# Whole-row gate and up weights in place of 512-column blocks, in the feed-forward tail of a decode kernel

## The chip, the cores and the metric

The kernel runs on one core of a Trainium2 chip. The metric is the time of one execution on the device in microseconds (us). Before the change the median of 4 runs is 473.97 us, with runs from 472.04 to 476.5. The profile is of one execution with a span of 470.3 us.

## The reference

The program is one decode step (one new token for each of 8 sequences) of a transformer block whose layer norms are modulated by a condition vector. It has two halves: attention over a cache of keys and values, and a gated feed-forward network (FFN). Cut to what matters:

```python
# B=8 tokens, D=1024, 32 query heads on 4 K/V heads, cache length 8192, head size 128, F=3584
mod = silu(c) @ w_mod                              # six vectors: sa, ca, ga, sb, cb, gb
h = layernorm(x) * (1 + ca) + sa
q = h @ wq
p = softmax(q @ k_cache^T * 128**-0.5)             # per batch and head
x = x + ga * ((p @ v_cache) @ wo)
h = layernorm(x) * (1 + cb) + sb
gate = h @ W_gate                                  # [8, 1024] @ [1024, 3584]
up = h @ W_up                                      # [8, 1024] @ [1024, 3584]
x = x + gb * ((relu(gate) * up) @ W_down)          # [8, 3584] @ [3584, 1024]
```

All large arrays are bf16. The caches are 32 pairs (8 sequences times 4 K/V heads) of a 2 MB K tile and a 2 MB V tile. W_gate, W_up and W_down have 7.34 MB each. Everything is read once: 185.6 MB.

## The kernel before

The engines run side by side and meet at semaphores. One queue, that of SyncE (SP), issues all loads in program order; a wait on it holds back every later load.

The attention loop goes over the 32 pairs. For each, PE transposes the K tile in 8 rounds (`T_round`, line 633), ACT and DVE copy the result out of PSUM, PE multiplies it with the query (`A_part`), DVE and ACT make the softmax, and PE multiplies with V (`D_step`, line 669). K and V have two slots each:

```python
def dma_v(i):
    b, g = pair_bg[i]
    s = i % NKV
    if i >= NKV:
        sp.wait_ge(ev_pv.sem, i - NKV + 1)            # D_step(i-2) done
    ...
    ev_dma_v[s].mark(sp.dma_start(V_sb[s], vsrc))

def dma_k(i):
    ...
    if i >= NKV:
        sp.wait_ge(ev_tround.sem, 8 * (i - NKV) + 8)  # transposes of i-2 done
    ev_dma_kt[s].mark(sp.dma_start(Kp_sb[s], ksrc))

for i in range(NPR):
    dma_k(i)
    if i >= 1:
        dma_v(i - 1)
    if i == NPR - 1:
        dma_v(i)
    if i == 1 and DO_MODB:
        dma_wmodB()
    if FULL and i % B == 3:
        dma_wo(g)
while ffn_issued[0] < len(ffn_blocks):                # after the last V
    dma_ffn(ffn_issued[0])
    ffn_issued[0] += 1
```

SBUF is laid out by hand in one arena of 192 KB per partition: RA (32 KB, output projection), RB (64 KB, first the query weights, then the second part of w_mod, which PE has used up early in the attention loop), RC (64 KB, the K and V slots), RKT (16 KB, the transposed K) and RD (16 KB, free).

The FFN weights are 21 blocks of 1 MB in the order gate, up, down for each of seven groups of 512 hidden columns. Each block has a slot of 8 KB per partition and a wait for whatever used the slot:

```python
if kind == "G":
    src = B_W_gate[:, fb * 512:(fb + 1) * 512].rearrange("(c p) f -> p c f", p=128)
elif kind == "U":
    src = B_W_up[:, fb * 512:(fb + 1) * 512].rearrange("(c p) f -> p c f", p=128)
else:
    src = B_W_down[fb * 512:(fb + 1) * 512, :].rearrange("(f p) d -> p f d", p=128)
ev_dma_ffn[blk].mark(sp.dma_start(ffn_view(blk), src))
```

PE works through the groups as they arrive, with gate and up of one group ahead of down of the group before. The weights are the stationary operand and the 8 tokens the moving one:

```python
def gate_up(fb):                                     # line 750
    for kind, coff in (("G", 0), ("U", 32)):
        pe.wait_ge(ev_dma_ffn[(kind, fb)].sem, 16)
        for f4 in range(4):
            for cc in range(NCH):                    # NCH = 8 chunks of the 1024 rows
                pe.matmul(PS[:, coff + f4 * B:...], wv[:, cc, f4 * 128:(f4 + 1) * 128],
                          h2T[:, cc, :], start=(cc == 0), stop=(cc == NCH - 1))
for fb in range(NFB + 1):                            # NFB = 7
    if fb < NFB:
        gate_up(fb)
    if fb >= 1:
        down(fb - 1)                                 # line 765, 32 matmuls
```

ACT applies the relu to each group's gate (line 419), DVE multiplies it with up (line 571) and adds up the results of `down` (line 565). At the end DVE makes the sum with the residual, PE transposes it, ACT copies it and SP stores it.

Of the kernel before, what the change touches and what calls it, by code (L numbers as in the profile page):

```python
# [4 lines left out]
F32 = mybir.dt.float32  # L5
ACTF = mybir.ActivationFunctionType
ALU = mybir.AluOpType
AX = mybir.AxisListType

B = 8  # L10
D = 1024
# [4 lines left out]
FF = 3584  # L16
REP = HQ // HKV
NCH = D // 128
NP = HKV * B
# [3 lines left out]
NFB = FF // 512  # L23
# [19 lines left out]
def bass_adaLN_cond__gqa_block_cached__glu_gated_reglu__decode_kernel(  # L43
# [15 lines left out]
    NPR = NP if FULL else DEBUG_NP  # L59
# [3 lines left out]
    KB = 1024  # L63
# [17 lines left out]
    RA = 0  # L81
    RB = 32 * KB
    RC = 96 * KB
    RKT = 160 * KB
    RD = 176 * KB
    NKV = 2
# [12 lines left out]

    ffn_blocks = []  # L100
    for fb in range(NFB):
        for kind in ("G", "U", "D"):
            ffn_blocks.append((kind, fb))
    last0 = max(i for i in range(NP) if i % NKV == 0)
    last1 = max(i for i in range(NP) if i % NKV == 1)
    ffn_slot_of = {}
    ffn_region_wait = {}
    tail_regions = [
        (KV_SLOT[0], ("T", last0)), (KV_SLOT[0] + 8 * KB, ("T", last0)),
        (KV_SLOT[1], ("T", last1)), (KV_SLOT[1] + 8 * KB, ("T", last1)),  # L110
        (RKT, ("A", NP - 1)), (RKT + 8 * KB, ("A", NP - 1)),
        (KV_SLOT[0] + 16 * KB, ("D", last0)), (KV_SLOT[0] + 24 * KB, ("D", last0)),
        (KV_SLOT[1] + 16 * KB, ("D", last1)), (KV_SLOT[1] + 24 * KB, ("D", last1)),
    ]
    for k, blk in enumerate(ffn_blocks):
        if k < 8:
            ffn_slot_of[blk] = RB + k * 8 * KB
            ffn_region_wait[blk] = ("modb", None)
        elif k < 10:
            ffn_slot_of[blk] = RD + (k - 8) * 8 * KB  # L120
            ffn_region_wait[blk] = ("free", None)
        elif k < 12:
            ffn_slot_of[blk] = RA + (k - 10) * 8 * KB
            ffn_region_wait[blk] = ("w", 3)
        else:
            off, wt = tail_regions[k - 12]
            ffn_slot_of[blk] = off
            ffn_region_wait[blk] = wt

    def ffn_view(blk):  # L130
        kind, fb = blk
        off = ffn_slot_of[blk]
        if kind == "D":
            return aview(off, [4, D])
        return aview(off, [NCH, 512])

    identb = nc.alloc_sbuf_tensor("identb", [128, 128], BF16)
# [29 lines left out]
    x1T = nc.alloc_sbuf_tensor("x1T", [128, NCH, B], F32)  # L167
    grelu = [nc.alloc_sbuf_tensor(f"grelu{k}", [128, 4, B], F32) for k in range(2)]
    hhT = nc.alloc_sbuf_tensor("hhT", [128, FF // 128, B], BF16)
# [10 lines left out]
    PS_W2 = nc.alloc_psum_tensor("psW2", [128, 512], F32)  # L180
    GU_BANK = [PS_W1, PS_W2]
    Y_OFF = 384
# [8 lines left out]
    ev_dma_wo = [Ev(nc, f"ev_dma_wo{h}", 16) for h in range(2)]  # L191
    ev_dma_ffn = {blk: Ev(nc, f"ev_dma_ffn_{blk[0]}{blk[1]}", 16) for blk in ffn_blocks}
    ev_out = Ev(nc, "ev_out", 16)
# [79 lines left out]
    with nc.Block() as block:  # L273
# [15 lines left out]
        def _(sp):  # L289
# [14 lines left out]

            ffn_issued = [0]

            def dma_ffn(k):
                blk = ffn_blocks[k]
                kind, fb = blk
                wk, wv = ffn_region_wait[blk]  # L310
                if wk == "modb":
                    sp.wait_ge(ev_pe_misc.sem, PE_MISC_MODB)
                elif wk == "free":
                    pass
                elif wk == "w":
                    sp.wait_ge(ev_w.sem, wv)
                elif wk == "T":
                    sp.wait_ge(ev_tround.sem, 8 * wv + 8)
                elif wk == "A":
                    sp.wait_ge(ev_qk.sem, wv + 1)  # L320
                else:
                    sp.wait_ge(ev_pv.sem, wv + 1)
                if kind == "G":
                    src = B_W_gate[:, fb * 512:(fb + 1) * 512].rearrange("(c p) f -> p c f", p=128)
                elif kind == "U":
                    src = B_W_up[:, fb * 512:(fb + 1) * 512].rearrange("(c p) f -> p c f", p=128)
                else:
                    src = B_W_down[fb * 512:(fb + 1) * 512, :].rearrange("(f p) d -> p f d", p=128)
                ev_dma_ffn[blk].mark(sp.dma_start(ffn_view(blk), src))  # L329

# [24 lines left out]
            for i in range(NPR):  # L355
                b, g = pair_bg[i]
                dma_k(i)
                if i >= 1:
                    dma_v(i - 1)
                if i == NPR - 1:  # L360
                    dma_v(i)
                if i == 1 and DO_MODB:
                    dma_wmodB()
                if FULL:
                    if i % B == 3:
                        dma_wo(g)
            if FULL:
                while ffn_issued[0] < len(ffn_blocks):
                    dma_ffn(ffn_issued[0])
                    ffn_issued[0] += 1  # L370
                sp.wait_ge(ev_act_misc.sem, ACT_MISC_OUT)
                ev_out.mark(sp.dma_start(out.rearrange("t o (c p) -> (t o c) p", p=128), out_sb[0:B * NCH, :]))
            else:
                if NPR > 0:
                    sp.wait_ge(ev_ao.sem, NPR)
                else:
                    sp.wait_ge(ev_dve_misc.sem, DVE_MISC_QT)
                if DO_MODB:
                    sp.wait_ge(ev_act_misc.sem, ACT_MISC_MODB)
                ev_out.mark(sp.dma_start(out.rearrange("b o d -> (b o) d"), xc_nl[0:B, :]))  # L380
# [3 lines left out]
        def _(act):  # L384
# [29 lines left out]
            ln_sqrt(2)  # L414
            for fb in range(NFB):
                act.wait_ge(ev_ffn1.sem, 2 * fb + 2)
                if fb >= 2:
                    act.wait_ge(ev_hh.sem, fb - 1)
                ins = act.activation(grelu[fb % 2][:, :, :], GU_BANK[fb % 2][:, 0:32].rearrange("p (f t) -> p f t", t=B),  # L419
                                     ACTF.Relu)  # L420
                assert ev_relu.mark(ins) == fb + 1
            act.wait_ge(ev_pe_misc.sem, PE_MISC_FIN)
# [3 lines left out]
        def _(dve):  # L426
# [131 lines left out]
            def o2_acc(fb):  # L558
# [7 lines left out]
                assert ev_o2.mark(ins_) == fb + 1  # L566

            for fb in range(NFB):
                dve.wait_ge(ev_ffn1.sem, 2 * fb + 2)
                dve.wait_ge(ev_relu.sem, fb + 1)  # L570
                ins = dve.tensor_tensor(hhT[:, fb * 4:(fb + 1) * 4, :], grelu[fb % 2][:, :, :],  # L571
                                        GU_BANK[fb % 2][:, 32:64].rearrange("p (f t) -> p f t", t=B), ALU.mult)
                assert ev_hh.mark(ins) == fb + 1
                if fb >= 1:
                    o2_acc(fb - 1)
            o2_acc(NFB - 1)

# [7 lines left out]
        def _(pe):  # L585
# [152 lines left out]

            def gate_up(fb):
                PS = GU_BANK[fb % 2]  # L740
                if fb >= 2:
                    pe.wait_ge(ev_hh.sem, fb - 1)
                for kind, coff in (("G", 0), ("U", 32)):
                    blk = (kind, fb)
                    pe.wait_ge(ev_dma_ffn[blk].sem, 16)
                    wv = ffn_view(blk)
                    ins_ = None
                    for f4 in range(4):
                        for cc in range(NCH):
                            ins_ = pe.matmul(PS[:, coff + f4 * B:coff + (f4 + 1) * B],  # L750
                                             wv[:, cc, f4 * 128:(f4 + 1) * 128],
                                             h2T[:, cc, :], start=(cc == 0), stop=(cc == NCH - 1))
                    assert ev_ffn1.mark(ins_) == 2 * fb + (1 if kind == "G" else 2)

            def down(fb):
                blk = ("D", fb)
                pe.wait_ge(ev_dma_ffn[blk].sem, 16)
                pe.wait_ge(ev_hh.sem, fb + 1)
                if fb >= 2:
                    pe.wait_ge(ev_o2.sem, fb - 1)  # L760
                wv = ffn_view(blk)
                ins_ = None
                for dc in range(NCH):
                    for f4 in range(4):
                        ins_ = pe.matmul(PS_S[fb % 2][:, dc * B:(dc + 1) * B], wv[:, f4, dc * 128:(dc + 1) * 128],
                                         hhT[:, fb * 4 + f4, :], start=(f4 == 0), stop=(f4 == 3))
                assert ev_ffn2.mark(ins_) == fb + 1

            for fb in range(NFB + 1):
                if fb < NFB:  # L770
                    gate_up(fb)
                if fb >= 1:
                    down(fb - 1)

# [33 lines left out]
```

## Time and profile before

| | |
|---|---|
| median of 4 runs | 473.97 us |
| span of the profiled execution | 470.3 us |
| PE busy | 357.2 us (76%) |
| DVE busy | 216.2 us (46%) |
| ACT busy | 122.9 us (26%) |
| bytes moved | 186.73 MB, mean 397 GB/s |
| transposes of K, line 633 | 2048 matmuls, 189.3 us |
| gate and up, line 750 | 448 matmuls, 13.8 us |

The page counts an engine as busy while it has an instruction in work, so the shares say how full it is, not what sets the end. The chain of waits goes back from the last instruction to what released it, and so on to the start; it names who held whom. The row of GB/s cuts the span in 40 slices of 11.76 us. A DMA issue takes little time on the queue itself (327 ns at line 353 for a K tile); the data land some 10 us later, and the page lists the time from issue to landing.

### The profile page before, as it was taken

The numbers are of one execution on the slowest core, as the hardware profiler recorded it, in microseconds if no ns is written. First come the engines' busy times: TensorE is split into PE (matmuls) and PEld (weight loads), VectorE is DVE, ScalarE is ACT, GpSimd is POOL, SyncE is SP. The second block draws the span as 40 slices with busy tenths as digits, with TensorE's granted clock in tenths as the row PEclk, the third lists the DMA queues.
The fourth block names the chain that finished last, engine by engine and source line by source line (L and its number), as shares of the span: only waits on it lengthen the run. The fifth ranks groups of instructions, "written<-read, shape, count | busy, mean of one in ns | idle before, by whom it ended". The sixth has DMA issues, their size and how long they took to land.

```text
span 470.3 us, 16776 instructions
## 1 busy us (share of the span) xinstructions
PE 357.2 (76%) x7897; PEld 336.3 (72%) x7897; DVE 216.2 (46%) x460; ACT 122.9 (26%) x148; POOL 1.2 (0%) x9
## 2 busy tenths in 40 slices
PE   0407915699999989999999989998989999664333
PEld 0307815688988879988888888888989888554323
DVE  0100713245666635675565656556655665620000
ACT  2100412033333413343333333233333333200000
POOL 1000000000000000000000000000000000000000
PEclk9999966678788865797887888678887887755555
DMA  7999999999999999999999999999999999999994
GB/s 303 421 429 429 413 427 425 405 357 398 371 426 426 420 421 413 388 386 425 419 419 419 404 427 422 428 421 392 396 414 422 425 423 408 370 359 362 364 357 147
DMA packets 35045, 186.73 MB, mean 397 GB/s; under 512 B 1680, under 2 KB 16016, under 8 KB 24736
## 3 DMA queue, kind: packets, MB, share of 16 engines
q1 hardware_dynamic: 34976, 185.65, 98.2%
q8 instruction: 62, 1.02, 0.9%
q14 instruction: 7, 0.06, 0.0%
HBM read 185.63 MB, written 0.02 MB: 395 GB/s over the span
## 4 chain that ended last, share of the span: by engine, by line
PE 53%; DMA 20%; DVE 13%; SPq 9%; issue 4%; ACT 1%
PE psX L633 26%; DMA arena<-in_A_k_cache_dram 11%; PE psS L669 10%; SPq L329 8%; DVE arena L270 7%; PE psS L649 7%; DMA arena<-in_A_wq_dram 6%; DVE psS L513 4%; DMA arena<-in_B_W_down_dram 3%; PE psM L661 2%; PE psS L672 2%; PE psW L615 2%; PE psW L694 2%; PE psW L683 1%; PE psM L656 1%
## 5 line engine op out<-in xcount | busy, mean ns | idle before, releaser
L633 PE MATMUL psX<-identb,arena 128*128 128x128 bf16 x2048 | 189.3, 257 | 17.1 <-DMA arena<-in_A_k_cache_dram 14.3
L633 PEld LDWEIGHTS psX<-identb,arena 128*128 128x128 bf16 x2048 | 156.7, 118 | 17.7 <-DMA arena<-in_A_k_cache_dram 14.6
L268 ACT COPY arena<-psX 128x1024 bf16<-128x1024 bf16 x96 | 97.2, 1012 | 267.6 <-PE psX L633 267.6
L270 DVE COPY arena<-psX 128x1024 bf16<-128x1024 bf16 x160 | 106.7, 683 | 63.1 <-PE psX L633 63.1
L649 PE MATMUL psS<-QT,arena 128*128 128x8 bf16 x2048 | 89.7, 168 | 16.8 <-DVE arena L270 15.6
L649 PEld LDWEIGHTS psS<-QT,arena 128*128 128x128 bf16 x2048 | 79.4, 100 | 28.7 <-DVE arena L270 23.1
L669 PE MATMUL psS<-PT,arena 128*128 128x8 bf16 x2048 | 57.9, 166 | 6.2 <-issue 3.5
L669 PEld LDWEIGHTS psS<-PT,arena 128*128 128x128 bf16 x2048 | 54.9, 97 | 7.2 <-issue 4.4
L520 DVE TENSOR_REDUCE PTsum<-PT 128x8 f32<-128x512 bf16 x32 | 34.1, 1066 | 1.9 <-ACT PT L400 1.9
L750 PE MATMUL psW<-h2T,arena 128*128 128x8 bf16 x448 | 13.8, 168 | 26.6 <-DMA arena<-in_B_W_gate_dram 14.7
L750 PEld LDWEIGHTS psW<-h2T,arena 128*128 128x128 bf16 x448 | 12.9, 104 | 27.6 <-issue 15.8
L484 DVE RECIPROCAL rrs<-psS 128x8 f32<-128x8 f32 x32 | 6.7, 208 | 49.2 <-PE psS L672 49.2
L513 DVE TENSOR_TENSOR psS<-psS,bc_sb 128x512 f32<-128x512 f32 x32 | 22.4, 699 | 1.1
L495 DVE TENSOR_REDUCE m<-psS 128x8 f32<-128x512 f32 x32 | 22.0, 686 | 0.4 <-PE psS L649 0.4
L400 ACT ACTIVATE PT<-psS 128x512 bf16<-128x512 f32 x32 | 19.3, 602 | 6.5 <-DVE psS L513 6.5
L615 PE MATMUL psW<-hT,arena 128*128 128x8 bf16 x256 | 7.2, 168 | 17.7 <-DMA arena<-in_A_wq_dram 15.5
L509 DVE COPY bc_sb<-psM 128x8 f32<-128x8 f32 x32 | 5.3, 167 | 32.4 <-PE psM L661 32.4
L615 PEld LDWEIGHTS psW<-hT,arena 128*128 128x128 bf16 x256 | 7.0, 104 | 17.9 <-DMA arena<-in_A_wq_dram 15.7
L571 DVE TENSOR_TENSOR hhT<-grelu,psW 128x32 bf16<-128x32 f32 x7 | 1.3, 188 | 39.1 <-ACT grelu L419 39.1
L661 PEld LDWEIGHTS psM<-diag,onesf 8*128 8x128 f32 x64 | 10.9, 213 | 5.5 <-issue 2.6
L661 PE MATMUL psM<-diag,onesf 8*128 8x8 f32 x64 | 13.8, 286 | 0.6 <-DVE diag L504 0.6
L672 PE MATMUL psS<-PTsum,onesf 128*128 128x8 f32 x64 | 13.9, 290 | 0.3 <-issue 0.3
(71 smaller groups left out, 126.2 us busy)
## 6 DMA issues: line engine op xcount, KB each, us to landing
arena<-in_A_k_cache_dram SPq DMA_DIRECT2D x32, 2048.0 KB, 10.8
arena<-in_A_v_cache_dram SPq DMA_DIRECT2D x32, 2048.0 KB, 12.5
arena<-in_w_mod_dram SPq DMA_DIRECT2D x6, 2048.0 KB, 13.6
arena<-in_A_wq_dram SPq DMA_DIRECT2D x4, 2048.0 KB, 24.9
arena<-in_A_wo_dram SPq DMA_DIRECT2D x4, 2048.0 KB, 17.4
arena<-in_B_W_gate_dram SPq DMA_DIRECT2D x7, 1024.0 KB, 11.8
arena<-in_B_W_up_dram SPq DMA_DIRECT2D x7, 1024.0 KB, 13.3
arena<-in_B_W_down_dram SPq DMA_DIRECT2D x7, 1024.0 KB, 12.7
```

Source lines behind the costliest of these rows:

```text
L268: ins_ = eng_api.copy(dst, src)
L270: ins_ = eng_api.tensor_copy(dst, src)
L329: ev_dma_ffn[blk].mark(sp.dma_start(ffn_view(blk), src))
L513: ins_ = dve.tensor_tensor(sview, sview, bcb, ALU.subtract)
L520: ins_ = dve.tensor_reduce(PTsum[:, :], PT[i % 2][:, :].rearrange("p (q h) -> p h q", h=REP), AX.X, ALU.add)
L615: ins = pe.matmul(PS_W2[:, h * B:(h + 1) * B], wq_sb[:, cc, h * DH:(h + 1) * DH], hT[:, cc, :], start=(cc == 0), stop=(cc == NCH - 1))
L633: ins_ = pe.transpose(x[:, j * 128:(j + 1) * 128], Kpq_sb[s_][:, q, :], identb[:, :])
L649: ins_ = pe.matmul(PS_S[i % 2][:, q * REP:(q + 1) * REP], KT3_sb[s_][:, q, :], QT[:, b, g * REP:(g + 1) * REP], start=True, stop=True)
L661: ins_ = pe.matmul(PS_M[:, 128:128 + REP], onesf[0:REP, :], diag[0:REP, :], start=True, stop=True)
L669: pe.matmul(PS_S[i % 2][:, 0:REP], Vq_sb[s_][:, q, :], PT[i % 2][:, q * REP:(q + 1) * REP], start=(q == 0), stop=(q == NQ - 1))
L672: ins_ = pe.matmul(PS_S[i % 2][:, REP:2 * REP], onesf[:, :], PTsum[:, :], start=True, stop=True)
L750: ins_ = pe.matmul(PS[:, coff + f4 * B:coff + (f4 + 1) * B], wv[:, cc, f4 * 128:(f4 + 1) * 128], h2T[:, cc, :], start=(cc == 0), stop=(cc ...
```

## The change

The gate and up weights are no longer loaded in blocks of 512 columns but in chunks of 128 whole rows of 3584 columns, 7 KB per partition and chunk, eight chunks for each matrix. They come in five transfers of two to five chunks. The down weights keep their seven blocks and get new places. The aim is to have longer contiguous pieces in each transfer, fewer transfers and waits, and part of the gate weights in SBUF ahead of the tail.

A chunk holds all columns for one eighth of the sum. So all eight chunks of gate are needed before any of its columns can be finished: PE now does the whole of gate, then the whole of up, then all of down, with one relu and one multiplication for all 3584 columns in place of seven.

The first two gate chunks lie in RD and are issued in step 4 of the attention loop. The next two are issued ahead of the last V tile. The last five up chunks lie in RC and wait for the last attention step.

```diff
+    CB = 7 * KB
+    Wg_23 = aview(RB, [2, FF])
+    Wg_47 = aview(RB + 2 * CB, [4, FF])
+    Wg_01 = aview(RD, [2, FF])
+    Wu_02 = aview(RB + 6 * CB, [3, FF])
+    Wu_37 = aview(RC, [5, FF])
+    wd_offs = [RC + 56 * KB, RKT, RKT + 8 * KB, RA, RA + 8 * KB, RA + 16 * KB, RA + 24 * KB]
+    wd_wait = [None, ("qk", None), ("qk", None), ("w", 3), ("w", 3), ("w", 4), ("w", 4)]
 ... (the table of the 21 blocks and dma_ffn(k) are removed)
+            srcg = B_W_gate.rearrange("(c p) f -> p c f", p=128)
+
+            def dma_ffn_all():
+                ev_dma_wg.mark(sp.dma_start(Wg_47, srcg[:, 4:8, :]))
+                srcu = B_W_up.rearrange("(c p) f -> p c f", p=128)
+                ev_dma_wu.mark(sp.dma_start(Wu_02, srcu[:, 0:3, :]))
 ... (last0 and last1: the last pairs of the two slots)
+                for lp in (last0, last1):
+                    if lp >= 0:
+                        sp.wait_ge(ev_tround.sem, 8 * lp + 8)
+                        sp.wait_ge(ev_pv.sem, lp + 1)
+                ev_dma_wu2.mark(sp.dma_start(Wu_37, srcu[:, 3:8, :]))
+                for k in range(NFB):
 ... (wait for wd_wait[k])
+                    srcd = B_W_down[k * 512:(k + 1) * 512, :].rearrange("(f p) d -> p f d", p=128)
+                    ev_dma_wd[k].mark(sp.dma_start(Wd_sb[k], srcd))
 ...
                 if i >= 1:
                     dma_v(i - 1)
+                if i == 4:
+                    ev_dma_wg.mark(sp.dma_start(Wg_01, srcg[:, 0:2, :]))
                 if i == NPR - 1:
+                    sp.wait_ge(ev_pe_misc.sem, PE_MISC_MODB)
+                    ev_dma_wg.mark(sp.dma_start(Wg_23, srcg[:, 2:4, :]))
                     dma_v(i)
 ... (ACT: one relu for all groups; DVE: one multiplication, then the seven sums of down)
-            def gate_up(fb):
 ...
+            for kind, wch, PS in (("G", Wg_c, PS_W1), ("U", Wu_c, PS_W2)):
+                if kind == "G":
+                    pe.wait_ge(ev_dma_wg.sem, 48)
+                else:
+                    pe.wait_ge(ev_dma_wu.sem, 16)
+                    pe.wait_ge(ev_dma_wu2.sem, 16)
+                for fc in range(FF // 128):
+                    for cc in range(NCH):
+                        ins_ = pe.matmul(PS[:, fc * B:(fc + 1) * B], wch[cc][:, 0, fc * 128:(fc + 1) * 128],
+                                         h2T[:, cc, :], start=(cc == 0), stop=(cc == NCH - 1))
 ...
-            for fb in range(NFB + 1):
-                if fb < NFB:
-                    gate_up(fb)
-                if fb >= 1:
-                    down(fb - 1)
+            for fb in range(NFB):
+                down(fb)
```

More of the change, by code (lines that the diff above doesn't have):

```diff
@@ L98, in bass_adaLN_cond__gqa_block_cached__glu_gated_reglu__decode_kernel @@
     KT3_sb = [KT3_shared for s in range(NKV)]
[L100 to L135, printed above, removed]
+    CB = 7 * KB
+    Wg_c = [aview(RD + cc * CB, [1, FF]) for cc in range(2)] + [aview(RB + cc * CB, [1, FF]) for cc in range(6)]
+    Wu_c = [aview(RB + (6 + cc) * CB, [1, FF]) for cc in range(3)] + [aview(RC + cc * CB, [1, FF]) for cc in range(5)]
+    Wg_23 = aview(RB, [2, FF])
[5 more added lines that the diff above has]
+    wd_wait = [None, ("qk", None), ("qk", None), ("w", 3), ("w", 3), ("w", 4), ("w", 4)]
+    Wd_sb = [aview(off, [4, D]) for off in wd_offs]
     identb = nc.alloc_sbuf_tensor("identb", [128, 128], BF16)
@@ L167, in bass_adaLN_cond__gqa_block_cached__glu_gated_reglu__decode_kernel @@
     x1T = nc.alloc_sbuf_tensor("x1T", [128, NCH, B], F32)
-    grelu = [nc.alloc_sbuf_tensor(f"grelu{k}", [128, 4, B], F32) for k in range(2)]
+    grelu = nc.alloc_sbuf_tensor("grelu", [128, FF // 128, B], F32)
     hhT = nc.alloc_sbuf_tensor("hhT", [128, FF // 128, B], BF16)
@@ L180, in bass_adaLN_cond__gqa_block_cached__glu_gated_reglu__decode_kernel @@
     PS_W2 = nc.alloc_psum_tensor("psW2", [128, 512], F32)
-    GU_BANK = [PS_W1, PS_W2]
     Y_OFF = 384
@@ L191, in bass_adaLN_cond__gqa_block_cached__glu_gated_reglu__decode_kernel @@
     ev_dma_wo = [Ev(nc, f"ev_dma_wo{h}", 16) for h in range(2)]
-    ev_dma_ffn = {blk: Ev(nc, f"ev_dma_ffn_{blk[0]}{blk[1]}", 16) for blk in ffn_blocks}
+    ev_dma_wg = Ev(nc, "ev_dma_wg", 16)
+    ev_dma_wu = Ev(nc, "ev_dma_wu", 16)
+    ev_dma_wu2 = Ev(nc, "ev_dma_wu2", 16)
+    ev_dma_wd = [Ev(nc, f"ev_dma_wd{k}", 16) for k in range(NFB)]
     ev_out = Ev(nc, "ev_out", 16)
@@ L303, in dma_wmodB @@
                     ev_dma_wmodB.mark(sp.dma_start(wmodB_sb[:, h * 2:(h + 1) * 2, :], srcB[:, h * 2:(h + 1) * 2, :]))
[L305 to L329, printed above, removed]
@@ new lines, in _ @@
+            srcg = B_W_gate.rearrange("(c p) f -> p c f", p=128)
[3 more added lines that the diff above has]
+                ev_dma_wu.mark(sp.dma_start(Wu_02, srcu[:, 0:3, :]))
+                last0 = max(i for i in range(NPR) if i % NKV == 0) if NPR > 0 else -1
+                last1 = max(i for i in range(NPR) if i % NKV == 1) if NPR > 1 else -1
+                for lp in (last0, last1):
[4 more added lines that the diff above has]
+                for k in range(NFB):
+                    wk = wd_wait[k]
+                    if wk is not None:
+                        if wk[0] == "qk":
+                            sp.wait_ge(ev_qk.sem, NPR)
+                        else:
+                            sp.wait_ge(ev_w.sem, wk[1])
+                    srcd = B_W_down[k * 512:(k + 1) * 512, :].rearrange("(f p) d -> p f d", p=128)
+                    ev_dma_wd[k].mark(sp.dma_start(Wd_sb[k], srcd))
@@ L367, in _ @@
             if FULL:
-                while ffn_issued[0] < len(ffn_blocks):
-                    dma_ffn(ffn_issued[0])
-                    ffn_issued[0] += 1
+                dma_ffn_all()
                 sp.wait_ge(ev_act_misc.sem, ACT_MISC_OUT)
@@ L414, in _ @@
             ln_sqrt(2)
[L415 to L421, printed above, removed]
+            act.wait_ge(ev_ffn1.sem, 1)
+            ins = act.activation(grelu[:, :, :], PS_W1[:, 0:FF // 128 * B].rearrange("p (f t) -> p f t", t=B),
+                                 ACTF.Relu)
+            assert ev_relu.mark(ins) == 1
             act.wait_ge(ev_pe_misc.sem, PE_MISC_FIN)
@@ L566, in o2_acc @@
                 assert ev_o2.mark(ins_) == fb + 1
-            for fb in range(NFB):
[L569 to L573, printed above, removed]
-                if fb >= 1:
-                    o2_acc(fb - 1)
-            o2_acc(NFB - 1)
+            dve.wait_ge(ev_ffn1.sem, 2)
+            dve.wait_ge(ev_relu.sem, 1)
+            ins = dve.tensor_tensor(hhT[:, :, :], grelu[:, :, :],
+                                    PS_W2[:, 0:FF // 128 * B].rearrange("p (f t) -> p f t", t=B), ALU.mult)
+            assert ev_hh.mark(ins) == 1
+            for fb in range(NFB):
+                o2_acc(fb)
             dve.wait_ge(ev_o2.sem, NFB)
@@ L737, in _ @@
             pe.wait_ge(ev_dve_misc.sem, DVE_MISC_H2)
-            def gate_up(fb):
[L740 to L753, printed above, removed]
+            for kind, wch, PS in (("G", Wg_c, PS_W1), ("U", Wu_c, PS_W2)):
+                if kind == "G":
+                    pe.wait_ge(ev_dma_wg.sem, 48)
+                else:
+                    pe.wait_ge(ev_dma_wu.sem, 16)
+                    pe.wait_ge(ev_dma_wu2.sem, 16)
+                ins_ = None
+                for fc in range(FF // 128):
+                    for cc in range(NCH):
+                        ins_ = pe.matmul(PS[:, fc * B:(fc + 1) * B], wch[cc][:, 0, fc * 128:(fc + 1) * 128],
+                                         h2T[:, cc, :], start=(cc == 0), stop=(cc == NCH - 1))
+                assert ev_ffn1.mark(ins_) == (1 if kind == "G" else 2)
             def down(fb):
-                blk = ("D", fb)
-                pe.wait_ge(ev_dma_ffn[blk].sem, 16)
-                pe.wait_ge(ev_hh.sem, fb + 1)
+                pe.wait_ge(ev_dma_wd[fb].sem, 16)
+                if fb == 0:
+                    pe.wait_ge(ev_hh.sem, 1)
                 if fb >= 2:
                     pe.wait_ge(ev_o2.sem, fb - 1)
-                wv = ffn_view(blk)
+                wv = Wd_sb[fb]
                 ins_ = None
@@ L767, in down @@
                 assert ev_ffn2.mark(ins_) == fb + 1
-            for fb in range(NFB + 1):
-                if fb < NFB:
-                    gate_up(fb)
-                if fb >= 1:
-                    down(fb - 1)
+            for fb in range(NFB):
+                down(fb)
             pe.wait_ge(ev_dve_misc.sem, DVE_MISC_FIN)
```

## The prediction

> **What bounds the kernel now.** I read the two DMA rows of the page first.
>
> ```profile
> DMA  7999999999999999999999999999999999999994
> GB/s 303 421 429 429 413 427 425 405 357 398 371 426 426 420 421 413 388 386 425 419 419 419 404 427 422 428 421 392 396 414 422 425 423 408 370 359 362 364 357 147
> DMA packets 35045, 186.73 MB, mean 397 GB/s; under 512 B 1680, under 2 KB 16016, under 8 KB 24736
> ```
>
> The DMA engines are busy from the first slice to the last, so the span is nearly bytes over rate. But the rate isn't one number: about 420 GB/s for most of the span, about 360 in slices 34 to 38, with the engines still busy. The packet line says why. One 512-column block of the gate or up weights has 1024 row pieces of 1024 bytes; 14 blocks make 14336 pieces, and 14336 + 1680 = 16016. So all packets between 512 B and 2 KB are the gate and up weights.
>
> Next the end of the chain of waits (start, length, what):
>
> ```profile
> 448.17 1.36 SPq L329
> 449.58 3.87 SPq L329
> 453.49 11.91 DMA arena<-in_B_W_down_dram
> 465.45 1.03 PE psS L765 x32
> ```
>
> The last transfer lands at 465.4, then comes one down block (1.03 us), and 470.3 - 465.4 = 4.9 us is all that follows the last byte. Nothing on PE or DVE holds the FFN up; it waits for weights. The timeline of PE in the tail gives the size of a block:
>
> ```profile
> 442.68 0.99 PE L750 MATMUL psW<-h2T,arena 128*128 128x8 bf16 x32 [3.98 <-DMA arena<-in_B_W_gate_dram]
> 445.59 1.02 PE L750 MATMUL psW<-h2T,arena 128*128 128x8 bf16 x32 [1.92 <-DMA arena<-in_B_W_up_dram]
> ...
> 451.43 0.99 PE L750 MATMUL psW<-h2T,arena 128*128 128x8 bf16 x32 [3.96 <-DMA arena<-in_B_W_gate_dram]
> ```
>
> One round of gate, up and down takes 451.43 - 442.68 = 8.75 us for 3 x 1.049 = 3.146 MB: 360 GB/s. The last down block came 2.57 us after the last up block (465.45 - 462.88), while up came 2.91 us after gate. I choose 2.75 us for a down block (2048-byte pieces) and so 6.0 us for a gate and an up block together (350 GB/s).
>
> Last, the table by stretch (columns: length, busy time of PE, PEld, DVE, ACT, POOL, then PEclk, DMA share, GB/s), and the DMA issues around the end of attention:
>
> ```profile
> 102.00:104.00 2.00, 1.68 (x40) 1.40 (x37) 1.68 (x3) 1.56 (x3) 0.00 (x0) 1.00 0.53 221
> 104.00:106.00 2.00, 1.76 (x64) 1.67 (x64) 1.12 (x2) 0.21 (x1) 0.00 (x0) 1.00 0.87 188
> 115.00:120.00 5.00, 5.00 (x103) 4.94 (x100) 2.43 (x6) 1.01 (x1) 0.00 (x0) 0.66 0.96 360
> 125.00:130.00 5.00, 5.00 (x104) 4.94 (x101) 2.61 (x7) 1.01 (x1) 0.00 (x0) 0.68 0.93 318
> 360.00:370.00 10.00, 9.20 (x222) 8.42 (x220) 7.50 (x16) 4.30 (x5) 0.00 (x0) 1.00 1.01 427
> 440.00:450.00 10.00, 2.87 (x96) 2.72 (x96) 0.41 (x2) 0.20 (x1) 0.00 (x0) 0.50 1.09 360
> ```
>
> ```profile
> 381.99 0.33 SPq L353 DMA_DIRECT2D arena<-in_A_k_cache_dram  x1
> 384.97 9.92 SPq L337 DMA_DIRECT2D arena<-in_A_v_cache_dram  x2
> 394.93 0.44 SPq L329 DMA_DIRECT2D arena<-in_B_W_gate_dram  x1
> ```
>
> Between 102 and 130 us the DMA engines have holes; in the tail they are over-full (1.09) and yet slow. The merged second line is V(30) at 385.0 and V(31) at 394.6; V(31) lands 9.1 us later, at 403.7. So the FFN stream runs from 403.7 to 465.4: 61.7 us for 22.0 MB.
>
> **What the Trainium skill says.** "DMA: Bandwidth & Descriptors", section "Why small descriptors are slow (HBM only)": each packet carries a fixed cost beside its bytes. The trace agrees: 350 GB/s with 1 KB pieces (my split), 427 where the caches come in 16 KB pieces. The section "Queues, rings and completion order" of the same page says that descriptors of one ring are consumed in order; the FFN blocks land in the order of their issue here, so I add transfers up one after the other. "Perfetto Trace Analysis", section "Roofline", puts the ceiling of a single core at its 16 DMA engines, about 435 GB/s; the best slices here have 429. So large pieces can at best bring the tail to about 420 to 429, and no more.
>
> **The change part by part.**
>
> *Pieces.* Gate and up now arrive as whole rows of 3584 columns, 7168 bytes: 2048 pieces for 14336. For the rate I take 420 GB/s, what the stretch from 10 to 30 us shows (423 and 418) while the query weights arrive in 8 KB pieces. 14.68 MB / 420 = 34.95 us against 7 x 6.0 = 42.0: 7.05 us saved. The down weights keep their pieces: 7 x 2.75 = 19.25 us.
>
> *Earlier start.* Two gate chunks (1.835 MB, 4.37 us) are issued in step i = 4, right after V(3), which went out at 86.2 us. V(3) lands 20.3 us later, at 106.5, its last part while other engines already idle (0.53 of the share at 102 to 104); those engines can go on with the new transfer. The four stretches shown lack, against 420: 0.40 + 0.46 + 0.30 + 0.51 = 1.67 MB, or 4.0 us. The first two alone hold 2.1 us. So K(5) lands at most about 2.3 us later than now: 112.5 + 2.3 = 114.8 (issue 103.44 plus 9.1), and its transposes start at 116.85. No wait. Later K tiles are issued 12 to 15 us ahead of their use and land in 10.8 (the page's median). I charge 0.5 us for the whole, not 4.37.
>
> *The order at the end of attention.* Two more gate chunks (1.835 MB) go ahead of V(31). It then lands at 403.7 + 4.37 = 408.1, and its 64 matmuls start at 410.0 now: still in time, by 1.9 us. Then the stream: gate chunks 4 to 7, 3.67 MB, 8.74 us, to 416.8; up chunks 0 to 2, 2.75 MB, 6.55 us, to 423.4; up chunks 3 to 7, 4.59 MB, 10.92 us, to 434.3; down, 19.25 us, to 453.5. The sum 4.37 + 8.74 + 6.55 + 10.92 + 19.25 is 49.8 us for 61.7: 11.9 us less.
>
> *The new wait.* Up chunks 3 to 7 overwrite K and V buffers and may not be issued before the last attention step is done, 412.3 now. The queue has work until 423.4, so this wait should be covered by 11 us.
>
> *Compute that no longer interleaves.* Gate runs when h2T is there (420.0), 224 matmuls at 28 ns (116 in 3.25 us at the granted 0.5): to 426.3. Up starts at 434.3 and ends at 440.6. The one multiplication on DVE has 224 columns; 512 take 699 ns at L513, so I estimate 0.35 us and with the hand-over 0.6: 441.2. By then two down blocks are there and the third is landing; at about 1 us each, PE has caught up before the fourth lands at 445.3. So only the last down block stays exposed, as now, and 4.9 us follow the last byte: 453.5 + 4.9 = 458.4, and with the 0.5 us above 458.9. That is 11.4 us off the span of 470.3. Off the median of 473.97 it gives 462.6 us (2.4% faster).
>
> **The rivals.**
>
> *The early chunks are paid in attention.* From 140 to 340 us the DMA share is 0.98 to 1.02 in every stretch of 20 us. If attention is bound by DMA and the holes don't take the 1.835 MB, everything after shifts by 4.4 us and only the pieces pay: 473.97 - 11.9 + 4.4 = 466.5. For it: the full share. Against: PE waits for K only three times, 14.3 us in all, of which 13.1 at 62 to 75 us.
>
> *The new wait makes a hole.* If the queue ran dry before 412.3, the whole barrier would show: V(31) late plus a later attention end. Each us of hole is a us of time. The margin of 11 us speaks against; a hole of 5 us would give 467.6.
>
> *Serial compute becomes the bound.* If up took twice as long (12.6 us), down would start at 447.5 with six blocks waiting and end near 455, 1 to 2 us late: about 464. The measured 28 ns speaks against it.
>
> *Piece size doesn't matter.* If the slow tail comes from the down rows or from HBM and not from 1 KB pieces, 7 us vanish and only the moved bytes stay: 469. The dip that begins with the first gate block speaks against.
>
> **Range and chances.** The centre is 462.6. Attention also swings with the granted clock (1.00 in some stretches of the table, 0.66 in others), and the runs before spread over 4.5 us. Full payment in attention makes 466.5; free early chunks and 427 GB/s make about 461.5; with a quiet clock 2 to 3 less. So 458.5 to 467.5. Two per cent is 464.5, only 1.9 us above the centre, so faster by over 2% gets 0.66, within 2% 0.30, slower 0.04.
>
> **What would show it.** Right: packets near 22757 (35045 - 12288) with only 1680 under 2 KB; GB/s about 420 until about 434 and about 380 after; no hole near 412; last down transfer landing near 454; the up matmuls starting when the second up transfer lands; T rounds near 117 us unshifted. Wrong: PE waiting for K between 110 and 150, attention ending later than 412 by 3 us or more, a drop of GB/s after 412, or the down blocks running back to back after the last byte.

## The result and the profile after

The changed kernel takes 464.03 us (median of 11 runs, 461.88 to 467.67) against 473.25 us (16 runs). The ratio is 0.9807, with a 95% interval of 0.9775 to 0.9839: about 9.1 us less, where the prediction had 11.4. The line of 2% lies inside the interval, so faster by over 2%, to which the prediction gave the best chance (0.66), is not decided. Ratios, here and below, leave out executions in a slower state of the chip; the medians in us do not. The profiled execution has a span of 461.3 us.

The DMA rows of the page after:

```profile
DMA  7999999999999999999999999999999999999992
GB/s 300 422 429 426 414 423 430 403 424 421 379 425 419 426 426 404 422 425 429 381 381 426 424 409 423 425 418 394 411 419 405 429 423 422 421 419 418 403 386 109
DMA packets 22612, 186.72 MB, mean 405 GB/s; under 512 B 1536, under 2 KB 1536, under 8 KB 12304
```

The shelf at 360 GB/s is gone: 418 to 422 in slices 33 to 36, then a step down to 386 for the down weights, which still come in 2 KB pieces. No packets of 1 KB are left (all under 2 KB are under 512 B), and there are 12433 packets fewer. Slice 8 (92 to 104 us here, 94 to 106 before) has 424 for 357 before.

The DMA issues around the end of attention (start, length, what):

```profile
381.72 0.33 SPq L326 DMA_DIRECT2D arena<-in_A_k_cache_dram  x1
384.92 0.33 SPq L310 DMA_DIRECT2D arena<-in_A_v_cache_dram  x1
385.29 0.43 SPq L337 DMA_DIRECT2D arena<-in_B_W_gate_dram  x1
396.43 0.33 SPq L310 DMA_DIRECT2D arena<-in_A_v_cache_dram  x1
...
414.07 0.37 SPq L293 DMA_DIRECT2D arena<-in_B_W_up_dram  x1
414.48 29.79 SPq L302 DMA_DIRECT2D arena<-in_B_W_down_dram  x7
```

The K tile and V(30) go out within 0.3 us of before (381.99 and 384.97). V(31) goes out 1.8 us later than before and lands 14.3 us after that, at 410.7. The last down block lands at 456.0. The up transfer that waits for attention goes out at 414.07. The chain of waits from there to the end:

```profile
414.07 22.84 DMA arena<-in_B_W_up_dram
436.91 0.14 issue
437.05 4.06 PE psW L718 x147
441.11 2.46 issue
443.56 2.21 PE psW L718 x77
...
446.33 1.50 PE psS L732 x51
447.83 2.11 issue
449.94 3.63 PE psS L732 x126
453.57 2.47 issue
456.05 1.43 PE psS L732 x47
```

Up and down are now in the chain as PE work, and between them stand three pauses of 2.1 to 2.5 us in which PE waits for nothing that the profile shows. They come after about 128 matmuls each (77 + 51, then 126). These pauses became the first question of the experiments.

### The profile page after: what moved, and what is told of

It reads as the page before. It is cut to its first block, busy times and chain, and to the rows that moved or that the text cites. A ratio compares the mean times of both kernels' runs of the same rounds, so it can differ in the third digit from the quotient of the medians.

```text
span 461.3 us, 16741 instructions
## 1 busy us (share of the span) xinstructions
PE 357.4 (77%) x7897; PEld 338.0 (73%) x7897; DVE 215.7 (47%) x454; ACT 121.9 (26%) x142; POOL 1.2 (0%) x9
## 3 DMA queue, kind: packets, MB, share of 16 engines
q8 instruction: 62, 1.02, 0.9%
## 4 chain that ended last, share of the span: by engine, by line
PE 55%; DMA 25%; DVE 11%; issue 6%; ACT 1%; SPq 1%
PE psX L603 27%; DMA arena<-in_A_k_cache_dram 14%; PE psS L639 9%; PE psS L619 7%; DMA arena<-in_A_wq_dram 6%; DVE arena L246 6%; DMA arena<-in_B_W_up_dram 5%; DVE psS L485 3%; PE psM L631 2%; PE psS L642 2%; PE psW L585 2%; PE psW L664 2%; PE psS L732 1%; PE psW L718 1%; PE psM L626 1%
## 5 line engine op out<-in xcount | busy, mean ns | idle before, releaser
L603 PE MATMUL psX<-identb,arena 128*128 128x128 bf16 x2048 | 191.9, 259 | 16.5 <-DMA arena<-in_A_k_cache_dram 15.0
L603 PEld LDWEIGHTS psX<-identb,arena 128*128 128x128 bf16 x2048 | 158.8, 119 | 17.5 <-DMA arena<-in_A_k_cache_dram 15.4
L639 PE MATMUL psS<-PT,arena 128*128 128x8 bf16 x2048 | 56.9, 166 | 5.4 <-issue 2.9
L718 PE MATMUL psW<-h2T,arena 128*128 128x8 bf16 x448 | 12.6, 168 | 12.5 <-DMA arena<-in_B_W_up_dram 7.8
L631 PEld LDWEIGHTS psM<-diag,onesf 8*128 8x128 f32 x64 | 10.9, 212 | 5.2 <-issue 2.1
L472 DVE TENSOR_REDUCE gmax<-psM 8x1 f32<-8x128 f32 x32 | 8.9, 277 | 9.8 <-PE psM L626 9.8
## 6 DMA issues: line engine op xcount, KB each, us to landing
arena<-in_A_v_cache_dram SPq DMA_DIRECT2D x32, 2048.0 KB, 13.6
arena<-in_B_W_down_dram SPq DMA_DIRECT2D x7, 1024.0 KB, 15.9
```

The lines of the kernel that those rows point to most:

```text
L603: ins_ = pe.transpose(x[:, j * 128:(j + 1) * 128], Kpq_sb[s_][:, q, :], identb[:, :])
L631: ins_ = pe.matmul(PS_M[:, 128:128 + REP], onesf[0:REP, :], diag[0:REP, :], start=True, stop=True)
L639: pe.matmul(PS_S[i % 2][:, 0:REP], Vq_sb[s_][:, q, :], PT[i % 2][:, q * REP:(q + 1) * REP], start=(q == 0), stop=(q == NQ - 1))
L718: ins_ = pe.matmul(PS[:, fc * B:(fc + 1) * B], wch[cc][:, 0, fc * 128:(fc + 1) * 128], h2T[:, cc, :], start=(cc == 0), stop=(cc == NCH - 1))
```

## The experiments

Each run is one alteration of the changed kernel, unless it says that it starts from another. Ratios are to the kernel before.

**Late chunks: the changed kernel without its early start.**

```diff
-                if i == 4:
-                    ev_dma_wg.mark(sp.dma_start(Wg_01, srcg[:, 0:2, :]))
             def dma_ffn_all():
+                ev_dma_wg.mark(sp.dma_start(Wg_01, srcg[:, 0:2, :]))
```

> Gate chunks 0 and 1 are issued after the last V tile instead of in step 4 of the attention loop; nothing else differs from the changed kernel. Theory (the early bytes travel in holes of the DMA and cost attention next to nothing): the whole tail moves back by the 4.4 us that 1.835 MB take, so about 468.4 us against 464.0, the last up transfer landing about 441 instead of 436.9. Rival (attention pays for the early bytes in full): within 1 us of 464.0, with attention ending about 4 us earlier than the 414.0 of the changed kernel.

Measured: 466.05 us, ratio 0.9849 (0.9824 to 0.9873). That is 0.0042 x 473 = 2.0 us more than the changed kernel: half of the 4.4, between theory and rival. The difference is itself uncertain by 1.9 us (an estimate from the two intervals), so it may be anything from 0.1 to 3.9. In its profile V(31) lands at 407.8, 2.9 us earlier than in the changed kernel, which also speaks for a part that attention pays.

**512-column pieces: the same order and places, other pieces.**

```diff
-                ev_dma_wg.mark(sp.dma_start(Wg_47, srcg[:, 4:8, :]))
+                dma_cols(ev_dma_wg, Wg_47, srcg, 4, 8)   # 7 transfers of 512 columns; all five likewise
```

> Gate and up go to the same places in the same order as in the changed kernel, but each transfer is cut into seven transfers of 512 columns, so that the pieces are 1 KB instead of 7 KB. Theory (piece size sets the rate of the tail): the 12.85 MB of gate and up that travel at the end take 36.8 us (7 x 6.0 us scaled by 12.85 / 14.68) instead of 30.6, so +6.2 us: about 470 us, GB/s near 350 between 410 and 440. Rival (the slow tail came from elsewhere): within 1 us of 464.0, GB/s staying at 416 to 422.

Measured: 469.5 us, ratio 0.9922 (0.99 to 0.9945), so 5.4 us more than the changed kernel. Its table by stretch (length, busy time of PE, PEld, DVE, ACT, POOL, then PEclk, DMA share, GB/s):

```profile
410.00:420.00 10.00, 5.39 (x134) 4.89 (x134) 3.19 (x10) 1.88 (x2) 0.00 (x0) 0.50 1.09 347
420.00:430.00 10.00, 5.53 (x177) 5.26 (x178) 2.04 (x10) 0.21 (x1) 0.00 (x0) 0.50 1.10 348
```

The changed kernel in the same stretches:

```profile
410.00:420.00 10.00, 5.04 (x134) 4.60 (x133) 3.96 (x13) 1.88 (x2) 0.00 (x0) 0.50 1.01 419
420.00:430.00 10.00, 6.96 (x226) 6.61 (x226) 1.27 (x6) 0.57 (x2) 0.00 (x0) 0.50 1.02 419
```

With places, order and consumers unaltered, the shorter pieces bring back the low rate and the over-full share. This run also has 35 transfers in place of five. The run with 8 KB down pieces below keeps the number of transfers and has longer pieces alone, and there too the rate rises. So piece size is what sped up the tail.

**Up in passes: less PE work after the last up transfer.**

```diff
-    Wu_37 = aview(RC, [5, FF])
+    Wu_34 = aview(RC, [2, FF])
+    Wu_57 = aview(RC + 2 * CB, [3, FF])
...
+            for ev_u, c0, c1 in ((ev_dma_wu, 0, 3), (ev_dma_wu2, 3, 5), (ev_dma_wu3, 5, 8)):
+                pe.wait_ge(ev_u.sem, 16)
+                for fc in range(FF // 128):
+                    for cc in range(c0, c1):
+                        ins_ = pe.matmul(PS_W2[...], Wu_c[cc][...], h2T[:, cc, :],
+                                         start=(fc == 0 and cc == 0), stop=(last of all))
```

> The last up transfer is cut in two (2 and 3 chunks) and PE multiplies up in three passes, as the chunks arrive, adding in PSUM; 84 matmuls of up instead of 224 are left after the last up transfer. Theory (PE is late at the end because it gets through only 128 matmuls in about 6.2 us, with a pause after each 128): down catches up with the weights before the last one lands, the time after the last landing falls from 8 to 5 us: about 461 us. Rival (the end is set by the DMA stream alone, and the 3 us beyond the expected 4.9 after it are something else, like a slow last hand-over): within 1 us of 464.0.

Measured: 463.44 us, ratio 0.9816 (0.9771 to 0.9861): no difference from the changed kernel. The end of its PE timeline shows why:

```profile
451.53 1.02 PE L738 MATMUL psS<-hhT,arena 128*128 128x8 bf16 x32 [1.66 <-DMA arena<-in_B_W_down_dram]
454.07 1.02 PE L738 MATMUL psS<-hhT,arena 128*128 128x8 bf16 x32 [1.52 <-DMA arena<-in_B_W_down_dram]
456.80 1.02 PE L738 MATMUL psS<-hhT,arena 128*128 128x8 bf16 x32 [1.71 <-DMA arena<-in_B_W_down_dram]
```

PE did catch up and waits for each down block, as the theory said; but there was hardly anything to win. My expectation rested on a misreading. I took the DMA share of 0.60 at 450 to 455 us in the changed kernel for the end of the stream at about 453. The time from issue to landing says otherwise: the last down block was issued at 440.1 and landed 15.9 us later, at 456.0, when PE was ready for it. A mean over engines falls before the slowest one is done. After the last landing the changed kernel needs 461.3 - 456.0 = 5.3 us, not 8.

**PE waits for all weights: the pauses without loads under way.**

```diff
                     pe.wait_ge(ev_dma_wg.sem, 48)
+                    for k in range(NFB):
+                        pe.wait_ge(ev_dma_wd[k].sem, 16)
```

> PE begins gate only when all FFN weights are in SBUF, so that gate, up and down, 672 matmuls, run while no load is under way. If the pauses after each 128 matmuls come from weights in flight crowding out the instructions, they shrink and the 672 matmuls take about 19 us (28 ns each): end near 478. If the rate of 128 in about 6.2 us is there without any load too, they take about 32 us: end near 491.

Measured: a single execution, 482.2 us, span 480.1. The same FFN matmuls in its PE timeline:

```profile
457.07 3.18 PE L720 MATMUL psW<-h2T,arena 128*128 128x8 bf16 x114 [35.01 <-DMA arena<-in_B_W_down_dram]
460.42 9.15 PE L720 MATMUL psW<-h2T,arena 128*128 128x8 bf16 x334 [0.17 <-issue]
470.15 6.12 PE L734 MATMUL psS<-hhT,arena 128*128 128x8 bf16 x224 [0.57 <-DVE hhT L542]
```

All 672 matmuls pass in 19.2 us, with no pause over 0.2 us apart from the hand-over to DVE. So the pauses come with loads in flight; they are not a limit of PE alone. Nor were the instructions all there beforehand: four instruction packets of 16 KB are loaded while these gate and up matmuls run (they start at 458.0, 461.5, 464.9 and 468.4), one for each 128 matmuls or so.

**The early start alone, on the kernel before.**

```diff
+        if k < 2:                                    # first gate and first up block
+            ffn_slot_of[blk] = RD + k * 8 * KB
...
+                if i == 4:
+                    dma_ffn(0)
+                    dma_ffn(1)
```

> The kernel before, with one alteration: the first gate block and the first up block (512 columns, 1 KB pieces, 2.1 MB) lie in RD and are issued in step 4 of the attention loop; the other blocks move up. It is the early start alone. Prediction as it stood (early bytes nearly free): two blocks of 3.0 us leave the tail for 0.5 us paid, so 5.5 us less than before, ratio about 0.988. Theory after the first experiments (late chunks cost 2.0 us of 4.4, so attention pays more than half): about 2.7 us less than before, ratio about 0.994.

Measured: 468.34 us, ratio 0.9891 (0.9852 to 0.993): 5.2 us less, near the prediction as it stood. The other theory (0.994) lies just outside the interval. Of the 6.0 us (estimated) that left the tail, attention kept 0.8 (-1.0 to 2.7).

**Down in 8 KB pieces.**

```diff
-  B_W_down[...].rearrange("(f p) d -> p f d", p=128)
+  B_W_down[...].rearrange("(p f) d -> p f d", f=4)
-  wch[cc][:, 0, fc * 128:(fc + 1) * 128]
+  wch[cc][:, 0, (fc // 4) * 512 + fc % 4:(fc // 4 + 1) * 512:4]
```

> In the changed kernel each down block is read with four consecutive rows per partition (pieces of 8 KB for 2 KB); to match, gate and up take every fourth column of a 512-column block as their stationary operand, so that the result is the same. The seven blocks should take 17.5 us (420 GB/s) for the 19.1 measured. Theory (PE with its pauses while weights are in flight is just behind the stream): the pauses hold the end where it is, gain under 0.7 us, about 463.6 us. Rival (DMA alone sets the end): 1.6 us less than the changed kernel, about 462.4.

Measured: 463.14 us, ratio 0.9787 (0.9737 to 0.9838). The gain over the changed kernel, 0.9 us by the ratios, is inside the intervals, so theory and rival can't be told apart. The stream is faster, 421 and 418 GB/s at 430 to 440 and 440 to 445 us, for 394 and 386 in the changed kernel:

```profile
430.00:440.00 10.00, 3.23 (x98) 3.17 (x97) 0.00 (x0) 0.36 (x1) 0.00 (x0) 0.50 1.02 421
440.00:445.00 5.00, 3.52 (x106) 3.46 (x105) 0.00 (x0) 0.00 (x0) 0.00 (x0) 0.50 1.01 418
```

But the end of PE's timeline stays where it was:

```profile
449.70 3.52 PE L732 MATMUL psS<-hhT,arena 128*128 128x8 bf16 x126 [1.28 <-issue]
456.10 1.42 PE L732 MATMUL psS<-hhT,arena 128*128 128x8 bf16 x47 [2.87 <-issue]
```

The sixth down block lands at 451.8 and the last at 455.8, 4.0 us later, for 2.4 or 2.5 us between the others. The DMA view narrows down why. From 453.8 us on it holds one piece of the weights alone, 8 KB at 454.6, and before that an instruction packet of 16 KB that starts at 453.5 and takes 1.1 us. So the last piece probably had to wait for the instruction packet; the view doesn't name the DMA engine, and no run tests it.

**8 KB down pieces and up in passes together.**

> The 8 KB down pieces together with up in three passes (last up transfer cut in two). Here PE has 84 matmuls of up left after the last up transfer instead of 224. Theory: with both, the 1.6 us of the stream come through: about 462.4 us, about 1.2 us under the run with the 8 KB pieces alone. Rival (PE isn't near the bound): the same as the 8 KB pieces alone.

Measured: 463.76 us, ratio 0.9781 (0.9736 to 0.9826): again not separable from the changed kernel. The profile has the shortest span, 460.0 us, and PE waits for DMA up to the last block:

```profile
452.72 1.02 PE L738 MATMUL psS<-hhT,arena 128*128 128x8 bf16 x32 [1.44 <-DMA arena<-in_B_W_down_dram]
455.18 1.01 PE L738 MATMUL psS<-hhT,arena 128*128 128x8 bf16 x32 [1.44 <-DMA arena<-in_B_W_down_dram]
```

From V(31) to the last byte this profile has 43.8 us (411.3 to 455.1), 1.5 less than the changed kernel. That is less than what these runs can tell apart.

**Gate and up chunks spread over attention** (on top of the run before).

```diff
+                if i >= 6 and i % 3 == 0:            # steps 6, 9, ... 30: one chunk each
+                    j = (i - 6) // 3
+                    if j < 6:
+                        ev_dma_wg.mark(sp.dma_start(Wg_c[2 + j], srcg[:, 2 + j:3 + j, :]))
+                    else:
+                        ev_dma_wu.mark(sp.dma_start(Wu_c[j - 6], srcu[:, j - 6:j - 5, :]))
```

> As the run before, and gate chunks 2 to 7 and up chunks 0 to 2 are no longer issued around the last V tile but one by one in attention steps 6, 9, 12 to 30 (0.918 MB each, 8.3 MB in all). If attention leaves holes in the DMA all along (its stretches average 413 to 419 GB/s where full ones have 425), the chunks fill them and the last landing moves forward by about 3 us: about 459.5 us. Rival (the queue is full and every byte is paid for in attention): the same as the run before within 1 us, with attention ending about 15 us later.

Measured: 472.16 us, ratio 0.9975 (0.9953 to 0.9997). The gain of the change is nearly gone, and neither the theory (459.5) nor the rival (within 1 us of the run before) had this. From the waits (engine, line, for what: us in all, times, longest) and the table by stretch:

```profile
PE psX L610 <- DMA arena<-in_A_k_cache_dram: 27.9, 9, 13.6
```

```profile
410.00:420.00 10.00, 8.58 (x175) 8.14 (x176) 5.82 (x13) 2.55 (x4) 0.00 (x0) 0.83 0.95 374
420.00:430.00 10.00, 6.29 (x170) 5.74 (x166) 5.33 (x11) 2.95 (x4) 0.00 (x0) 0.70 0.12 49
430.00:440.00 10.00, 5.55 (x133) 5.03 (x134) 3.30 (x16) 0.21 (x1) 0.00 (x0) 0.50 0.85 332
```

Two rivals of the prediction are seen here at once. Attention pays: PE waits for K 27.9 us for 13.6 in the run before, and the last attention step ends at 430.2 instead of 414.2, 16.0 us for the 19.8 us that 8.3 MB take at 420 GB/s. And the barrier makes a hole: all gate chunks and the first up chunks are loaded by then, so nothing is left to carry while SP waits for attention, and the DMA stands nearly idle at 49 GB/s for about 10 us.

**One load more, in step 4 and in step 18** (on the kernel before).

```diff
+                if i == 4:                           # the second run: 18
+                    ev_extra.mark(sp.dma_start(extra_sb, srcx[:, 0:2, :]))
```

> The kernel before, with one load more: in step 4 of the attention loop the two gate chunks (1.835 MB, rows 0 to 255 of the gate weights) are read into RD, and nobody uses them; the tail is the old one, with its 21 blocks. It measures what the early bytes cost by themselves. Prediction as it stood (they travel in holes): about 0.5 us more than before. Full payment: 4.4 us more. From the run with late chunks (2.0 of 4.4 us gained): about 2.4 us more, ratio about 1.005.

> The same extra load, in step 18 of the attention loop instead of step 4. In the middle of attention the DMA has no hole as at 100 to 130 us, and 8.3 MB spread over steps 6 to 30 made attention end 16 us later (82% of their 19.8 us). Theory (it depends on where the holes are): about 3.6 us more than before, ratio about 1.008, and more than in step 4. Rival (the queue is the same all along): the same as in step 4 within 1 us.

Measured: in step 4 the ratio is 1.0029 (0.9993 to 1.0066), 1.4 us more than the kernel before; in step 18 it is 1.0104 (1.0047 to 1.0161), 4.9 us more. The same bytes cost 1.4 us (-0.3 to 3.1) in one place and 4.9 us (2.2 to 7.6), which takes in their full 4.4, in the other. The intervals overlap at their ends; the difference of 3.5 us is just beyond its own uncertainty of 3.2 (an estimate from the two). The table by stretch of the kernel before, of the run with the load in step 4 and of the one with the load in step 18, in this order:

```profile
100.00:120.00 20.00, 18.64 (x390) 17.64 (x388) 12.61 (x25) 7.34 (x9) 0.00 (x0) 0.83 0.93 365
```

```profile
100.00:120.00 20.00, 17.97 (x380) 16.92 (x379) 12.00 (x23) 6.72 (x9) 0.00 (x0) 0.81 0.99 393
```

```profile
100.00:120.00 20.00, 18.11 (x383) 16.84 (x380) 12.46 (x25) 7.28 (x9) 0.00 (x0) 0.83 0.93 347
```

With the load in step 4 the hole at 100 to 120 us is filled: 393 GB/s at a share of 0.99, for 347 to 365 at 0.93 without it. The changed kernel has 395 there, and the run with late chunks 349.

## Why the prediction was right, and where it was off

*Piece size.* Right, and shown by the 512-column run: 5.4 us for the 6.2 expected. The tail runs at 419 (420 predicted) with whole rows and at 347 (350 predicted) with 1 KB pieces.

*The order after V(31).* Right to within 0.2 us a step, in one profile. From the landing of V(31) at 410.7, gate chunks 4 to 7 took 8.8 us (8.74), up chunks 0 to 2 took 6.5 (6.55), up chunks 3 to 7 took 10.9 (10.92) and down 19.1 (19.25). From V(31) to the last byte it is 45.3 us, for 45.4 in the prediction.

*The early start.* The bytes do travel more cheaply there, but "I charge 0.5 us for the whole" was most likely too little. It counted four holes of 1.67 MB between 102 and 130 us as if all could be filled. Against the run with late chunks, the stretch from 100 to 140 carries (410 - 383) x 40 us = 1.1 MB more, three fifths of the 1.835 MB. The times of three runs put the cost of early bytes at 2.4 us (4.4 less the 2.0 of the run with late chunks), 0.8 (the early start alone) and 1.4 (the extra load in step 4). Each is uncertain by 1.7 to 1.9 us; together they speak for about 1.5, but none clearly excludes 0.5. The landings are clearer. K(5), which was to land at 114.8 at the latest, lands at 115.4 in the changed kernel, and at 115.4 to 116.7 in seven other profiles with an early load; in the three without one it lands at 112.5 to 113.2.

The prediction also looked for the cost in one place alone, a PE that waits for K. PE didn't wait for K(5) in the changed kernel, yet the transposes of K(5) began at 119.77 for 116.85. Of these 2.9 us, 2.1 were there already when those of K(4) began (109.00 for 106.94), and most of that is longer pauses of PE in which it waits for nothing that the profile shows:

```profile
89.66 3.56 PE L664 MATMUL psW<-siluT,arena 128*128 128x8 bf16 x128 [2.27 <-issue]
96.13 1.95 PE L664 MATMUL psW<-siluT,arena 128*128 128x8 bf16 x68 [2.91 <-issue]
108.34 0.38 PE L639 MATMUL psS<-PT,arena 128*128 128x8 bf16 x8 [0.94 <-issue]
```

The kernel before has 1.33, 2.64 and 0.33 in these places, 1.8 us less in all. The extra load in step 4 shows the same (2.50, 2.92 and 0.99), but over all profiles with an early load the first two pauses come to 4.0 to 6.0 us, for 4.0 to 4.2 without. So how much of the cost runs over PE's pauses and how much over late K and V tiles stays open. That the cost depends on the place is what the extra load in step 18 shows.

*V(31).* Predicted at 408.1, or 408.6 with the charge; it landed at 410.7. V(30), issued at the same time as before, landed at 400.4 for 398.6: attention's stream was 1.8 us late there. (In the run with late chunks it landed at 398.6 too.) The remaining 0.9 us arose between V(30) and V(31). In the four other profiles with this order and 7 KB pieces (up in passes, all weights waited for, and the two with 8 KB down pieces) the two land 9.3 to 9.4 us apart, as the prediction had it, so the 0.9 belongs to this one execution. V(31) was still in time for its matmuls at 411.67.

*The new wait.* Right: no hole at 414; the queue had work until 426.0, 12 us longer. The spread run shows what that cover was worth.

*Serial compute.* Wrong, with little harm. The step that failed is "224 matmuls at 28 ns". The 28 ns hold within a run of matmuls, but not across the pauses: up took 8.7 us (437.05 to 445.77) instead of 6.3, and PE caught up at the last down block, not before the fourth. The last landing was 456.0 and the end 5.3 us later, for 4.9: 0.4 us. The profile of the kernel before had the pauses, in a stretch I didn't read closely enough, the second part of the modulation weights:

```profile
85.38 1.72 PE L694 MATMUL psW<-siluT,arena 128*128 128x8 bf16 x60
88.43 3.55 PE L694 MATMUL psW<-siluT,arena 128*128 128x8 bf16 x128 [1.33 <-issue]
94.63 1.96 PE L694 MATMUL psW<-siluT,arena 128*128 128x8 bf16 x68 [2.64 <-issue]
```

128 matmuls in 6.2 us from start to start, with loads under way: 48 ns each. That row belonged in the sum.

The sum: the last landing came at 456.0 for 453.5 + 0.5, 2.0 us late, as V(31) was, and the end another 0.4 us, from the pauses. Together 2.4 us of span, 458.9 predicted and 461.3 measured. That the pauses cost so little is in part luck: the third one ended at 456.05, just after the last block had landed at 456.0.

## What to carry to other kernels

Before a load is moved forward, look for the holes in the DMA share at the place where it will travel: here the same 1.835 MB cost 1.4 us in one step and 4.9 us in another. A transfer that must wait for a barrier needs other transfers queued ahead of it that keep the DMA engines at work meanwhile; those moved early no longer serve as cover. And take the end of a stream from the landing of its last transfer, not from a mean share.

## What the runs showed of the hardware

PE pauses after 128 matmuls while loads are in flight: 2.1 to 2.5 us in up and down of the changed kernel, so that 128 take about 6.2 us, but 0.5 us in its gate. Without loads it hardly pauses (0.2 us). With its weight load each matmul is two instructions, so 128 are 256 instructions. The Trainium skill, "Runtime: NRT & Kernel Launch", section "Instruction fetch mechanics", says that instructions are refilled in blocks of 256, 16 KiB, and calls the cost mostly hidden. The page's instruction queue fits the blocks (62 packets, 1.02 MB), and so does their time. In the changed kernel one instruction packet starts at 441.1, 447.3 and 453.7, 6.2 and 6.4 us apart, each within 0.5 us of the start of one of the three pauses; without loads they come about 3.5 us apart. So the trace shows that the cost is not hidden under load, and the measurement decides. That the fetch waits behind the weights is likely by these times and by the run that waits for all weights, but no run shows where it waits: the packet itself takes 1.0 to 1.1 us under load and 0.9 to 1.1 without.

Taking every fourth column as the stationary operand is slower: 147 matmuls of up took 5.04 us in the run with 8 KB down pieces, for 4.06 us with adjacent columns, 34 ns for 28.
